# A spectral mixing layer with a gated feed-forward block: half spectrum as symmetric and antisymmetric channel parts, and three matmul passes per mirrored pair

## The chip, the cores and the metric

The kernel runs on one core of one Trainium2 chip. The metric is the device time of one execution in microseconds (us); the median of several executions is quoted. Most executions of one kernel here agree within 0.1%. Matmul inputs are bf16 (but for the folding of the weights in the change, which is fp32), sums are fp32, and the output is fp32.

Names of the engines in the profile: PE is the matmul engine, PEld its weight loads (they overlap with PE), DVE the vector engine, ACT the scalar engine, POOL the general engine that issues loads, SP the engine whose queue (SPq) issues stores.

## The reference

```python
# x: 8 x 3008 x 256
X = np.fft.fft(x, axis=1)            # over the 3008 positions
X = np.fft.fft(X, axis=2)            # over the 256 channels
y = X.real.reshape(24064, 256)
g = y @ w_gate                       # 256 -> 1536
gelu = 0.5 * g * (1 + erf(g / sqrt(2)))
out = (gelu * (y @ w_val)) @ w_out   # 1536 -> 256
```

Both kernels do the transform as matmuls: 3008 is factored as 47 x 64, and the channel transform is a product with a 256 x 256 table of cosines or sines. "Layer 1" below is the two products with w_gate and w_val, "layer 2" the product with w_out, "a feature block" 128 of the 1536 features (there are 12), and "the product" the elementwise gelu times value on DVE.

## The kernel before

For each batch it has five stages on PE: a 64-point transform over positions, 66 transposes on PE that turn the result, a 47-point transform, the channel transform (cosine part U and sine part V), and the feed-forward block. Because the input is real, only 33 of the 64 groups are computed; U + V gives one position and U - V the mirrored one. Both are written to SBUF, and the feed-forward block then treats all 3008 positions alike.

```python
# transposes, 8 per PSUM buffer: 94 elements of A with a step of K1H = 33
src = _sub(A, [[N2 * K1H, 2], [K1H, N2]], cc * AST + k1)
nc.tensor.transpose(pst[:, idx * 128 : idx * 128 + 128], src, ident)
...
# channel transform: direct and mirrored positions from U and V
nc.scalar.activation(vsb[:, :N], psV[:, :N], AF.Copy)
nc.vector.tensor_tensor(dstD, psU[:, :N], vsb[:, :N], op=ALU.add)
...
nc.vector.tensor_tensor(dstM, psU[:, off : off + Nm], vsb[:, off : off + Nm], op=ALU.subtract)
...
# layer 1, one feature block of a chunk of 512 positions: 2 + 2 matmuls
for t in range(NCH):
    nc.tensor.matmul(psg[:, :ntok], Wg_sb[:, t, fc*128:(fc+1)*128],
                     Yt[:, t, u0:u0+ntok], start=(t == 0), stop=(t == NCH - 1))
...                                    # the same into psv with Wv_sb
nc.scalar.activation(gl[:, :ntok], psg[:, :ntok], AF.Gelu)
nc.vector.tensor_tensor(h[:, fc, :ntok], gl[:, :ntok], psv[:, :ntok], op=ALU.mult)
...
# layer 2: 12 matmuls of 256 columns for 128 positions, then one store
# for each run of at most 47 positions
```

The order of the instructions on each engine is fixed when the kernel is built, but it is not exactly the order of the program: in the trace single layer-2 matmuls stand between those of layer 1, where the program has twelve in a row.

Of the kernel before, what the change touches and what calls it, by code (L numbers as in the profile page):

```python
# [27 lines left out]

@with_exitstack
def kernel(  # L30
# [12 lines left out]
    N1, N2 = 64, 47  # L43
    K1H = 33
    NCH = C // 128
    NFC = F // 128
    AST = 2 * N2 * K1H
    DIR = K1H * N2

    TOK = 512  # L50
    chunk_sizes = []
    t0 = 0
    while t0 < T:
        chunk_sizes.append(min(TOK, T - t0))
        t0 += TOK
    NCHUNKS = len(chunk_sizes)

    const_pool = ctx.enter_context(tc.tile_pool(name="const", bufs=1))
    psum_pool = ctx.enter_context(tc.tile_pool(name="psum", bufs=1, space=bass.MemoryType.PSUM))

    G2 = const_pool.tile([128, 24, 2 * 66], BF16)
    T_PQ = const_pool.tile([2 * N2, 2 * N2], BF16)
    C2_sb = const_pool.tile([128, NCH, C], BF16)
    S2_sb = const_pool.tile([128, NCH, C], BF16)
    ident = const_pool.tile([128, 128], BF16)
    Wg_sb = const_pool.tile([128, NCH, F], BF16)
    Wv_sb = const_pool.tile([128, NCH, F], BF16)
    Wo_sb = const_pool.tile([128, NFC, C], BF16)

    scr_a = const_pool.tile([128, 24, K1H], FP32)  # L70
    scr_b = const_pool.tile([128, 24, K1H], FP32)
    scr_c = const_pool.tile([128, 24, K1H], FP32)
    scr_d = const_pool.tile([128, 24, K1H], FP32)
    col_a = const_pool.tile([128, 1], FP32)
    col_b = const_pool.tile([128, 1], FP32)
    col_c = const_pool.tile([128, 1], FP32)
    row_j = const_pool.tile([128, 24], FP32)
    row_t = const_pool.tile([128, 24], FP32)
    row_k = const_pool.tile([128, K1H], FP32)

    work_pool = ctx.enter_context(tc.tile_pool(name="work", bufs=1))
# [3 lines left out]
    def x_tile():  # L85
        return work_pool.tile([128, 24, C], BF16, tag="x", bufs=2, name="x_sb")

    def load_x(b, groups=None):
        xt = x_tile()
        x_tiles.append(xt)  # L90
        if groups is None:
            groups = [(j0, 3) for j0 in range(0, 24, 3)]
        for (j0, gj) in groups:
            src = ap_replace(
                x,
                ap=[[N2 * C, N1], [C, gj], [1, C]],
                offset=x.offset + (b * T + j0) * C,
            )
            nc.gpsimd.dma_start(out=xt[0:N1, j0 : j0 + gj, :], in_=src)  # L99
            gj2 = min(gj, 23 - j0)  # L100
            if gj2 > 0:
                src = ap_replace(
                    x,
                    ap=[[N2 * C, N1], [C, gj2], [1, C]],
                    offset=x.offset + (b * T + 24 + j0) * C,
                )
                nc.gpsimd.dma_start(  # L107
                    out=_sub(xt, [[C, gj2], [1, C]], j0 * C, part_start=N1, part_num=N1),
                    in_=src,
                )  # L110

    def A_tile():
        return work_pool.tile([128, NCH, 2, N2, K1H], BF16, tag="A", bufs=1, name="A_sb")

    def Ap_tile():
        return work_pool.tile([2 * N2, K1H, C], BF16, tag="Ap", bufs=1, name="Ap_sb")

    def PQ_tile():
        return work_pool.tile([128, NCH, K1H, 2, N2], BF16, tag="PQ", bufs=1, name="PQ_sb")

    def Y_tile():
        return work_pool.tile([128, NCH, T], BF16, tag="Y", bufs=2, name="Y_sb")

    def h_tile():
        return work_pool.tile([128, NFC, TOK], BF16, tag="h", bufs=2, name="h_sb")

    def gelu_tile():
        return work_pool.tile([128, TOK], BF16, tag="gelu", bufs=3, name="gelu_sb")

    def osb_tile():  # L130
        return work_pool.tile([128, C], FP32, tag="osb", bufs=4, name="out_sb")

    def vsb_tile():
        return work_pool.tile([128, 10 * N2], BF16, tag="vsb", bufs=2, name="v_sb")

    def ps_l1():
        return psum_pool.tile([128, TOK], FP32, tag="l1", bufs=3, name="ps_l1")

    def ps_o():
        return psum_pool.tile([128, 2 * C], FP32, tag="o", bufs=1, name="ps_o")  # L140

    def ps_dft():
        return psum_pool.tile([128, 512], FP32, tag="dft", bufs=3, name="ps_dft")

    def ps_tr():
        return psum_pool.tile([2 * N2, 1024], BF16, tag="tr", bufs=1, name="ps_tr")

    nc.gpsimd.iota(col_a, pattern=[[0, 1]], base=0, channel_multiplier=1,
                   allow_small_or_imprecise_dtypes=True)
    nc.gpsimd.iota(row_j, pattern=[[1, 24]], base=0, channel_multiplier=0,  # L150
                   allow_small_or_imprecise_dtypes=True)
    nc.gpsimd.iota(row_k, pattern=[[1, K1H]], base=0, channel_multiplier=0,
                   allow_small_or_imprecise_dtypes=True)
    load_x(0, groups=[(0, 1), (1, 1), (2, 1)] + [(j0, 3) for j0 in range(3, 24, 3)])
    for w_hbm, w_sb in ((moe_w_gate, Wg_sb), (moe_w_val, Wv_sb)):
        for q in range(4):
            src = ap_replace(
                w_hbm,
                ap=[[F, 32], [128 * F, NCH], [1, F]],
                offset=w_hbm.offset + q * 32 * F,  # L160
            )
            nc.gpsimd.dma_start(
                out=_sub(w_sb, [[F, NCH], [1, F]], 0, part_start=q * 32, part_num=32),
                in_=src,
            )
    for q in range(4):
        src = ap_replace(
            moe_w_out,
            ap=[[C, 32], [128 * C, NFC], [1, C]],
            offset=moe_w_out.offset + q * 32 * C,  # L170
        )
        nc.gpsimd.dma_start(
            out=_sub(Wo_sb, [[C, NFC], [1, C]], 0, part_start=q * 32, part_num=32),
            in_=src,
        )
    make_identity(nc, ident)

    nc.vector.memset(_sub(G2, [[1, 3 * 132]], 0), 0.0)
    nc.vector.memset(_sub(G2, [[1, 21 * 132]], 3 * 132), 0.0)
    nc.vector.tensor_scalar(col_b, col_a, 64.0, -2984.0, op0=ALU.is_ge, op1=ALU.mult)  # L180
    nc.vector.scalar_tensor_tensor(col_c, col_a, 47.0, col_b, op0=ALU.mult, op1=ALU.add)
    nc.vector.tensor_scalar(row_t, row_j, col_c, 1.0 / T, op0=ALU.add, op1=ALU.mult)

    def g2_group(j0, nj):
        for j in range(j0, j0 + nj):
            nc.vector.tensor_scalar(scr_a[:, j, :], row_k, row_t[:, j : j + 1], None, op0=ALU.mult)
        pha = _sub(scr_a, [[K1H, nj], [1, K1H]], j0 * K1H)
        tmp = _sub(scr_b, [[K1H, nj], [1, K1H]], j0 * K1H)
        nc.vector.tensor_scalar(tmp, pha, MAGIC, None, op0=ALU.add)
        nc.vector.scalar_tensor_tensor(  # L190
            _sub(scr_c, [[K1H, nj], [1, K1H]], j0 * K1H), tmp, MAGIC, pha,
            op0=ALU.subtract, op1=ALU.subtract)
        for half in range(2):
            p0 = half * 64
            cb = half * 66
            nc.scalar.activation(
                _sub(G2, [[132, nj], [1, K1H]], j0 * 132 + cb + K1H, part_start=p0, part_num=64),
                _sub(scr_c, [[K1H, nj], [1, K1H]], j0 * K1H, part_start=p0, part_num=64),
                AF.Sin, scale=TWO_PI,
            )  # L200
        nc.vector.tensor_scalar(pha, pha, 0.25, None, op0=ALU.add)
        nc.vector.tensor_scalar(tmp, pha, MAGIC, None, op0=ALU.add)
        nc.vector.scalar_tensor_tensor(
            _sub(scr_d, [[K1H, nj], [1, K1H]], j0 * K1H), tmp, MAGIC, pha,
            op0=ALU.subtract, op1=ALU.subtract)
        for half in range(2):
            p0 = half * 64
            cb = half * 66
            nc.scalar.activation(  # L209
                _sub(G2, [[132, nj], [1, K1H]], j0 * 132 + cb, part_start=p0, part_num=64),  # L210
                _sub(scr_d, [[K1H, nj], [1, K1H]], j0 * K1H, part_start=p0, part_num=64),
                AF.Sin, scale=-TWO_PI,
            )

    g2_group(0, 3)
    g2_group(3, 9)
    g2_group(12, 12)

    def gen_tpq():
        pcol = col_a  # L220
        rifl = _sub(col_b, [[1, 1]], 0, part_num=2 * N2)
# [38 lines left out]

    rowk2_94 = const_pool.tile([2 * N2, 2, N2], FP32)
    qrow_94 = const_pool.tile([2 * N2, 2, N2], FP32)
    row256 = const_pool.tile([128, C], FP32)

    Y_bufs = [None] * B

# [317 lines left out]
```

## Time and profile before

Before: 1007.57 us, median of 4 runs (1007.52 to 1008.25).

The first two lines and the summary of the chain of waits on the page of the kernel before. The second line gives busy microseconds, share of the span and instruction count for each engine.

```profile
span 1006.3 us, 17363 instructions
...
PE 950.6 (94%) x6218; PEld 611.2 (61%) x6304; DVE 611.0 (61%) x1209; ACT 489.7 (49%) x941; POOL 76.7 (8%) x157
...
PE 86%; ACT 4%; DMA 4%; DVE 2%; issue 1%; SPq 1%; POOL 1%; ACTq 0%; POOLq 0%
```

PE is the limit: it is busy for 94% of the span, and 86% of the chain that ended last is PE.

Groups of instructions of the kernel before, by line. The columns are line, engine and operation, output and inputs with shapes, count, then busy us and mean ns of one, then idle time before them.

```profile
L479 PE MATMUL ps_o<-Wo_sb,h_sb 128*128 128x256 bf16 (+1 forms) x2304 | 296.2, 272 | 5.2 <-ACT out_sb L487 1.4
...
L329 PEld LDWEIGHTS <-A_sb 128*94 128x94 bf16 x528 | 94.3, 252 | 14.8 <-issue 9.4
L329 PE MATMUL ps_tr<-ident,A_sb 128*94 128x128 bf16 x528 | 90.9, 318 | 9.9 <-DVE Ap_sb L337 5.7 <-POOL ident masks.py:199 3.7
```

The mean time of one matmul includes its latency, since matmuls are pipelined; the time that matters is from one start to the next. The transposes stand out: their weight loads take 252 ns against about 100 for the others.

Long pieces of the chain of waits of the kernel before, in order of time: start, duration, what.

```profile
90.78 1.47 PE ps_o L479 x12
...
209.29 1.49 PE ps_o L479 x12
...
327.82 1.49 PE ps_o L479 x12
...
446.34 1.49 PE ps_o L479 x12
```

The same layer-2 group comes back every 118.5 us. That is the period of one batch, and the kernel's time is a start, eight batches and a tail.

Windows of the kernel before around its end: the stretch, its length, then busy time and count of each engine, clock, DMA share of 16 engines and GB/s. The clock is the share of full speed that PE was granted.

```profile
960.00:988.00 28.00, 26.24 (x168) 16.07 (x165) 12.27 (x20) 12.78 (x26) 0.00 (x0) 1.00 0.10 34
988.00:1006.00 18.00, 0.23 (x3) 0.00 (x0) 0.00 (x0) 0.38 (x1) 0.00 (x0) 0.60 0.08 26
```

The last 18 us are stores, at 26 GB/s; the last matmul ends at 988.2.

### The profile page before, as it was taken

To read this page: it belongs to the slowest core of one execution; us is meant where nothing else is said; L and a number is where in the kernel's file an instruction comes from. 1 tells how busy PE (TensorE), PEld (TensorE's weight loads), DVE (VectorE), ACT (ScalarE), POOL (GpSimd) and SP (SyncE) were. 2 spreads that over 40 slices of the span, in tenths; PEclk is the share of its full clock that TensorE was granted. 3 is DMA by queue.
4 is the path that set the end of the run, shared out by engine and by line. 5 is a ranking of instruction groups with operands and counts; after the bars stand their busy time and mean duration, and the time that the engine had idled before them with its cause. 6 is when DMAs were issued, how large, how long until landed. Compare 5 with 4: busy or idle time off the path is not lost.

```text
span 1006.3 us, 17363 instructions
## 1 busy us (share of the span) xinstructions
PE 950.6 (94%) x6218; PEld 611.2 (61%) x6304; DVE 611.0 (61%) x1209; ACT 489.7 (49%) x941; POOL 76.7 (8%) x157
## 2 busy tenths in 40 slices
PE   3699999999999999999999999999999999999992
PEld 2646666557655676566765577656765667555551
DVE  5566656675566647757575756667467564765550
ACT  4254544554455454545445554454445545455550
POOL 7600300003000020002100030000000000000000
PEclk9999999999999999999999999999999999999997
DMA  8901411015100151013210150101010110001110
GB/s 137 142 1 30 77 38 29 24 29 84 29 30 27 28 84 29 26 28 64 51 30 23 31 84 28 30 27 29 23 29 29 25 31 23 29 22 31 33 34 27
DMA packets 40190, 40.45 MB, mean 40 GB/s; under 512 B 5544, under 2 KB 39592, under 8 KB 40104
## 3 DMA queue, kind: packets, MB, share of 16 engines
q0 software_dynamic: 12800, 14.69, 9.9%
q1 hardware_dynamic: 27304, 24.65, 8.6%
q8 instruction: 49, 0.80, 0.3%
q14 instruction: 37, 0.30, 0.1%
HBM read 29.36 MB, written 24.64 MB: 54 GB/s over the span
## 4 chain that ended last, share of the span: by engine, by line
PE 86%; ACT 4%; DMA 4%; DVE 2%; issue 1%; SPq 1%; POOL 1%; ACTq 0%; POOLq 0%
PE ps_o L479 24%; PE ps_tr L329 8%; DMA out_dram<-out_sb 2%; PE ps_dft L389 2%; PE ps_dft L397 2%; ACT gelu_sb L463 2%; PE ps_dft L361 1%; ACT out_sb L487 1%; PE ps_dft L282 1%; SPq L508 1%; DMA Wg_sb<-in_moe_w_gate_dram 1%; DVE h_sb L464 1%; ACT Ap_sb L334 0%; DMA x_sb<-in_x_dram 0%; DVE PQ_sb L369 0%
## 5 line engine op out<-in xcount | busy, mean ns | idle before, releaser
L479 PE MATMUL ps_o<-Wo_sb,h_sb 128*128 128x256 bf16 (+1 forms) x2304 | 296.2, 272 | 5.2 <-ACT out_sb L487 1.4
L479 PEld LDWEIGHTS <-h_sb 128*128 128x128 bf16 (+1 forms) x2304 | 225.9, 99 | 72.1 <-issue 11.6
L455 PEld LDWEIGHTS <-Wv_sb 128*128 128x128 bf16 x1152 | 113.3, 99 | 113.7 <-issue 3.2
L487 ACT ACTIVATE out_sb<-ps_o 128x256 f32<-128x256 f32 x192 | 73.7, 384 | 204.1 <-PE ps_o L479 192.5
L446 PEld LDWEIGHTS <-Wg_sb 128*128 128x128 bf16 x1152 | 109.3, 98 | 99.1 <-issue 32.4
L329 PEld LDWEIGHTS <-A_sb 128*94 128x94 bf16 x528 | 94.3, 252 | 14.8 <-issue 9.4
L329 PE MATMUL ps_tr<-ident,A_sb 128*94 128x128 bf16 x528 | 90.9, 318 | 9.9 <-DVE Ap_sb L337 5.7
L303 DVE CAST A_sb<-ps_dft 128x198 bf16<-128x198 f32 (+2 forms) x254 | 75.2, 342 | 21.7 <-PE ps_dft L282 16.5
L99 POOL DMA_DIRECT2D x_sb<-in_x_dram x66 | 36.7, 556 | 514.6 <-PE ps_dft L290 386.4
L334 ACT ACTIVATE Ap_sb<-ps_tr 94x512 bf16<-94x512 bf16 (+1 forms) x72 | 40.1, 557 | 67.1 <-PE ps_tr L329 67.1
L337 DVE COPY Ap_sb<-ps_tr 94x512 bf16<-94x512 bf16 (+1 forms) x72 | 28.5, 396 | 66.7 <-ACT Ap_sb L334 66.7
L369 DVE CAST PQ_sb<-ps_dft 128x470 bf16<-128x470 f32 (+1 forms) x112 | 67.5, 612 | 1.8 <-PE ps_dft L361 1.8
L282 PE MATMUL ps_dft<-G_61,x_sb 128*128 128x132 bf16 x368 | 45.1, 231 | 12.5 <-ACT G_61 L209 10.1
L407 DVE TENSOR_TENSOR Y_sb<-ps_dft,v_sb 128x470 bf16<-128x470 f32 (+1 forms) x64 | 35.8, 560 | 29.5 <-ACT v_sb L405 29.5
L282 PEld LDWEIGHTS <-x_sb 128*128 128x128 bf16 x368 | 31.8, 102 | 32.0 <-DMA x_sb<-in_x_dram 8.1
L361 PEld LDWEIGHTS <-Ap_sb 94*128 94x128 bf16 x528 | 35.4, 103 | 20.5 <-issue 1.6
L361 PE MATMUL ps_dft<-T_PQ,Ap_sb 94*128 94x94 bf16 x528 | 41.5, 214 | 2.6 <-ACT T_PQ L241 1.0
L405 ACT ACTIVATE v_sb<-ps_dft 128x470 bf16<-128x470 f32 (+1 forms) x64 | 31.6, 494 | 22.4 <-PE ps_dft L397 15.7
L107 POOL DMA_DIRECT2D x_sb<-in_x_dram x66 | 36.9, 559 | 6.4 <-DMA x_sb<-in_x_dram 2.6
L389 PE MATMUL ps_dft<-PQ_sb,C_sb 128*128 128x470 bf16 (+1 forms) x128 | 35.0, 337 | 1.9 <-DVE Y_sb L418 0.7
L397 PE MATMUL ps_dft<-PQ_sb,S_sb 128*128 128x470 bf16 (+1 forms) x128 | 35.0, 336 | 0.0
L418 DVE TENSOR_TENSOR Y_sb<-ps_dft,v_sb 128x470 bf16<-128x470 f32 (+2 forms) x64 | 34.0, 531 | 0.0
(2358 smaller groups left out, 1460.2 us busy)
## 6 DMA issues: line engine op xcount, KB each, us to landing
out_dram<-out_sb SPq DMA_DIRECT2D x328, 47.0 KB
x_sb<-in_x_dram POOLq DMA_DIRECT2D x118, 96.0 KB, 5.4
Wg_sb<-in_moe_w_gate_dram POOLq DMA_DIRECT2D x4, 192.0 KB, 6.5
Wv_sb<-in_moe_w_val_dram POOLq DMA_DIRECT2D x4, 192.0 KB, 8.2
Wo_sb<-in_moe_w_out_dram POOLq DMA_DIRECT2D x4, 192.0 KB, 7.5
x_sb<-in_x_dram POOLq DMA_DIRECT2D x8, 64.0 KB, 5.3
out_dram<-out_sb SPq DMA_DIRECT2D x8, 46.0 KB
out_dram<-out_sb SPq DMA_DIRECT2D x8, 45.0 KB
```

Of the source, the lines that this page charges most:

```text
L282: nc.tensor.matmul(ps[:, jj * 132 : (jj + 1) * 132], xt[:, j, cc * 128 : (cc + 1) * 128], G2[:, j, :], start=True, stop=True,)
L303: nc.vector.tensor_copy(dst, src)
L329: nc.tensor.transpose(pst[:, idx * 128 : idx * 128 + 128], src, ident)
L334: nc.scalar.activation(dst, pst[:, :h1], AF.Copy)
L361: nc.tensor.matmul(ps[:, j * 94 : (j + 1) * 94], Ap[:, k1, cc * 128 : (cc + 1) * 128], T_PQ, start=True, stop=True,)
L369: nc.vector.tensor_copy(dst, ps[:, : g * 94])
L389: nc.tensor.matmul(psU[:, :N], C2_sb[:, t, cpj * 128 : (cpj + 1) * 128], _sub(PQ, [[2 * N2, g], [1, N2]], t * AST + a * 2 * N2), start=(t ...
L397: nc.tensor.matmul(psV[:, :N], S2_sb[:, t, cpj * 128 : (cpj + 1) * 128], _sub(PQ, [[2 * N2, g], [1, N2]], t * AST + a * 2 * N2 + N2), star ...
L446: nc.tensor.matmul(psg[:, :ntok], Wg_sb[:, t, fc * 128 : (fc + 1) * 128], Yt[:, t, u0 : u0 + ntok], start=(t == 0), stop=(t == NCH - 1),)
L455: nc.tensor.matmul(psv[:, :ntok], Wv_sb[:, t, fc * 128 : (fc + 1) * 128], Yt[:, t, u0 : u0 + ntok], start=(t == 0), stop=(t == NCH - 1),)
L479: nc.tensor.matmul(pso[:m, col0 : col0 + C], h[:, fc, sub * 128 : sub * 128 + m], Wo_sb[:, fc, :], start=(fc == 0), stop=(fc == NFC - 1),)
L487: nc.scalar.activation(osb[:m], pso[:m, col0 : col0 + C], AF.Copy)
```

## The change

The intent: the real part of the spectrum at a position and at its mirror are E + O and E - O, where E is symmetric in the channels and O antisymmetric. So 128 rows hold all of E and 128 rows all of O (row 0 of the O tile carries one extra symmetric channel). The weights are folded once, at the start, into W_E and W_O. Layer 1 of a position is then W_E E + W_O O. For its mirror one does not start afresh: a third matmul adds W_M O, with W_M = -2 W_O (and 0 in the row of the extra symmetric channel), onto the bank that already holds the first sum. That is three passes for two positions instead of four. The transform itself becomes 94-row stage-1 matmuls, the channel transform, and a 64-point stage whose outputs are E and O; its order makes the transposes unnecessary.

```diff
-                    src = _sub(A, [[N2 * K1H, 2], [K1H, N2]], cc * AST + k1)
-                    nc.tensor.transpose(pst[:, idx * 128 : idx * 128 + 128], src, ident)
 ...
+        for (nm, q) in folds:                       # 6 pieces, at the start
+            nc.tensor.matmul(ps, exch, w_hi[nm][:, fs], start=True, stop=True)      # fp32
+            nc.vector.scalar_tensor_tensor(W[nm,"E"][:, fs], ps, keep, lo, op0=ALU.mult, op1=ALU.add)
+            nc.vector.scalar_tensor_tensor(W[nm,"O"][:, fs], lo, keep, ps, op0=ALU.mult, op1=ALU.subtract)
+            nc.vector.tensor_scalar(W[nm,"M"][:, fs], W[nm,"O"][:, fs], keep2, None, op0=ALU.mult)
 ...
-                for t in range(NCH):
-                    nc.tensor.matmul(psg[:, :ntok], Wg_sb[...], Yt[...], ...)
+    # l1_first(ci, fc): chunk of 512 (or 481) positions of the half spectrum
+                for nm, ps in (("g", pg), ("v", pv)):
+                    nc.tensor.matmul(ps[:, :n], W[nm,"E"][:, fs], EO[:, 0, c0:c0+n], start=True, stop=False)
+                    nc.tensor.matmul(ps[:, :n], W[nm,"O"][:, fs], EO[:, 1, c0:c0+n], start=False, stop=True)
+                nc.scalar.activation(gl[:, :n], pg[:, :n], AF.Gelu)
+                nc.vector.tensor_tensor(h[:, fc, 0, :n], gl[:, :n], pv[:, :n], op=ALU.mult)
+    # l1_second(ci, fc): the mirrored positions, in the same two banks
+                for nm, ps in (("g", pg), ("v", pv)):
+                    nc.tensor.matmul(ps[:, :n], W[nm,"M"][:, fs], EO[:, 1, c0:c0+n], start=False, stop=True, ...)
+                nc.scalar.activation(gl[:, :n], pg[:, :n], AF.Gelu)
+                nc.vector.tensor_tensor(h[:, fc, 1, n-1::-1], gl[:, :n], pv[:, :n], op=ALU.mult)
 ...
+    # a feature block's slot: first[fc], transform of the next batch ("filler"),
+    # second[fc-1], layer 2 of the chunk before ("pend")
 ...
-                    ap=[[N1 * C, ln], [1, C]]                   # store: ln <= 47 positions
+                    ap=[[C, n2], [N2 * C, hi - lo], [1, C]]     # store: n2 = 2 times 64 positions
 ...
-                ap=[[N2 * C, N1], [C, gj], [1, C]]              # load of x: 64 partitions
+                ap=[[NJ * C, NP], [1, nj * C]]                  # load of x: NP = 94 partitions
```

(The code lines are shortened, and the rest of the new transform and of its tables is cut.) PSUM: two banks for gate, two for value, two for layer 2, two for the transform.

## The prediction

> **What bounds it now.** TensorE. The page gives PE busy 950.6 us of a span of 1006.3 (94%), DVE 61%, ACT 49%, and the chain of waits is 86% PE. Three parts: a start of 56 us before layer 1, eight batches, a store tail (last matmuls at 988, end at 1006). In the timeline the same layer-2 group returns every 118.6 us (90.8, 209.3, 327.8, 446.3): one batch.
>
> **Cost of one batch on PE.** Start-to-start times in the timeline: 512 columns 215 ns, 256 columns 109 ns, 132 columns 58 ns, transposes 162 ns. The first three agree with the Trainium skill ("TensorE: Matmul & The Clock Gate", Back-to-back issue gap: N/2.4 + 2.5 ns warm). Layer 1 (288 matmuls) 61 us, layer 2 (288) 31.4, transposes (66) 10.8, the rest of the transform about 11: 114 us. The other 4.5 us (4%) are stalls.
>
> **Removed, added, moved.** Layer 1 falls from 288 matmuls over 3008 columns to 216 over 1505 mirrored columns: 45.7 us by the same rule, saving 15. The transposes go (10.8 us). New transform: 64 matmuls of 96 columns, 48 of 256, 24 of 64 and 24 of 128: about 11 us, equal to the old one without transposes. Layer 2 stays at 31.4. Sum 88 us a batch, 26 less.
>
> Nothing moves off PE: gelu (597 ns for 512) and the product (687 ns) stay 72 of each. DVE per batch: 49 us of products plus about 15 of PSUM copies = 65; ACT: 43 of gelu plus about 15 = 58.
>
> New dependency: a gate/value bank pair is now held through matmul, gelu, product, correction matmul, gelu, product. By the durations about 2.7 us for the value bank; with two banks 1.35 us per feature block at best, against 2.45 us of PE work; but in program order the block's 1.8 us of DVE work lies in that loop (2.5 us with matmul latency). So I expect more stalls than now: 6-7%, 94 us per batch.
>
> **Ends.** Start: the transform of batch 0 needs all of x, and its load uses 94 partitions. The Trainium skill ("DMA: Bandwidth & Descriptors", Why a DMA increments its semaphore by 16) says a DMA uses the largest number of engines up to 16 that divides the outer dimensions, so 2 for 94; no run here shows it. The weights (fp32) load beside it, then are folded on DVE. I estimate first layer 1 at 50 us, and 5 us lost waiting for batch 1's x. Tail: 26 large stores a batch instead of 87 small ones; 6 us after the last matmul instead of 18.
>
> **Sum:** 50 + 5 + 7 x 94 + 81 (last batch, no transform beside it) + 6 = 800 us; 8 in 10 between 772 and 845. Faster by over 2%: 0.97, within 2%: 0.02, slower: 0.01.
>
> **What would show it.** Period of a layer-2 group 92-97 us; PE still above 90% busy in mid-span; layer-1 matmul count 1728; no transposes; DVE about 70% busy, ACT about 62%; SP queue issues about 208. If the bank loop binds, PE's waits will name DVE products and ACT gelu, and the period will be over 100.
>
> **What would make it wrong.** The bank loop binding (period 100-105, total 850 or more); x arriving late over few DMA engines (start 65 or later, stalls at each batch's first transform); strided PSUM reads or 4-byte writes in the stage-1 copy slower than 0.55 us; a better overlap than I assume (period 90, total 770).

## The result, and the profile after

After: 781.16 us, median of 4 runs (780.76 to 781.40), against 1007.57 before in the same session. The ratio is 0.7751 (95% interval 0.7740 to 0.7762). Ratios here are the mean time of one kernel's fast runs over that of the other's in the same rounds, so they are not quite the ratio of the medians quoted.

The same lines of the page of the kernel after:

```profile
span 779.6 us, 13835 instructions
...
PE 736.1 (94%) x5324; PEld 478.9 (61%) x5324; DVE 496.7 (64%) x872; ACT 437.8 (56%) x823; POOL 12.7 (2%) x29
...
PE 85%; DVE 5%; ACT 4%; issue 2%; DMA 1%; SPq 0%; ACTq 0%; POOL 0%; POOLq 0%; DVEq 0%
```

PE is the limit as before, with the same busy share. Groups of the kernel after, by line:

```profile
L461 PE MATMUL ps_o<-Wo_sb,h_sb 128*128 128x256 bf16 (+1 forms) x2304 | 298.4, 273 | 0.0
...
L425 PE MATMUL ps_g<-EO_sb,WgE 128*128 128x512 bf16 (+1 forms) x288 | 107.8, 374 | 2.9 <-ACT gelu_sb L445 0.4
...
L441 PE MATMUL ps_g<-EO_sb,WgM 128*128 128x512 bf16 (+1 forms) x288 | 108.3, 376 | 0.8 <-ACT gelu_sb L428 0.7
```

Layer 2 is what it was. Layer 1 has six such groups of 288 (E, O and M, for gate and value): 1728 matmuls instead of 2304. The transposes are gone. The chain of waits in order of time:

```profile
89.58 1.31 PE ps_o L461 x12
...
179.81 1.31 PE ps_o L461 x12
...
270.03 1.31 PE ps_o L461 x12
```

The period is 90.2 us. Windows of the kernel after, for one load of x in mid-span, and around the end (columns as above):

```profile
168.60:180.30 11.70, 11.67 (x83) 7.90 (x81) 7.80 (x13) 6.14 (x11) 0.00 (x0) 1.00 0.73 141
756.00:765.00 9.00, 7.00 (x65) 6.32 (x62) 0.00 (x0) 1.19 (x2) 0.00 (x0) 1.00 0.14 48
765.00:774.00 9.00, 0.00 (x0) 0.00 (x0) 0.00 (x0) 0.60 (x1) 0.00 (x0) 0.57 0.20 64
774.00:780.00 6.00, 0.00 (x0) 0.00 (x0) 0.00 (x0) 0.00 (x0) 0.00 (x0) 0.50 0.08 28
```

While x is loaded, 0.73 of 16 engines are busy, that is 11.7 (the few stores of this stretch are counted too). Near the end, from 756 to 765, 0.14 of 16, that is 2.2, move 48 GB/s; PE works until 763.0 and then has nothing left to do, while 0.20 and then 0.08 of 16 engines (3.2 and 1.3) finish the stores. The end of the chain of waits of the kernel after shows the same:

```profile
755.18 0.61 ACT out_sb L470
...
755.80 0.51 SPq L407
...
756.36 9.48 DMA out_dram<-out_sb
...
765.95 0.60 ACT out_sb L470
```

The last copy of layer 2 on ACT needs a buffer that a store gives free; this store takes 9.5 us, and the copy starts at 765.95, 2.9 us after the last matmul.

The terms of the predicted sum beside the trace (first layer-1 matmul, end of the last matmul, end of the span):

| part | predicted, us | trace of after, us |
|---|---|---|
| start, to the first layer-1 matmul | 50 | 45.1 |
| from there to the end of the last matmul | 744 (5 + 7 x 94 + 81) | 717.9 |
| tail, to the end of the span | 6 | 16.6 |
| sum | 800 | 779.6 |

The period of the middle batches, taken from the first product of one batch to that of the next (the mean of six), is 90.33 us after and 118.57 before. If one adds N/2.4 + 2.5 ns for each matmul of a batch of the kernel after, the sum is 87.1 us; the start-to-start times of the trace, which has every matmul in this run, exceed that by 3.2 us a batch. This excess is what is left to stalls.

### The profile page after: what moved, and what is told of

Read it like the earlier page. It is cut to its first block, busy times and chain, and to the rows that moved or that the text cites. A ratio compares the mean times of both kernels' runs of the same rounds, so it can differ in the third digit from the quotient of the medians.

```text
span 779.6 us, 13835 instructions
## 1 busy us (share of the span) xinstructions
PE 736.1 (94%) x5324; PEld 478.9 (61%) x5324; DVE 496.7 (64%) x872; ACT 437.8 (56%) x823; POOL 12.7 (2%) x29
## 4 chain that ended last, share of the span: by engine, by line
PE 85%; DVE 5%; ACT 4%; issue 2%; DMA 1%; SPq 0%; ACTq 0%; POOL 0%; POOLq 0%; DVEq 0%
PE ps_o L461 30%; PE ps_g L425 9%; PE ps_v L425 8%; PE ps_v L426 8%; PE ps_g L426 7%; PE ps_v L441 7%; PE ps_g L441 7%; PE ps_dft L314 6%; PE ps_dft L285 3%; ACT gelu_sb L445 2%; DMA out_dram<-out_sb 1%; DVE h_sb L447 1%; PE ps_dft L356 1%; DVE h_sb L429 1%; ACT out_sb L470 1%
## 5 line engine op out<-in xcount | busy, mean ns | idle before, releaser
L429 DVE TENSOR_TENSOR h_sb<-gelu_sb,ps_v 128x512 bf16<-128x512 bf16 (+1 forms) x288 | 195.0, 677 | 204.2 <-ACT gelu_sb L428 132.4
L428 ACT ACTIVATE gelu_sb<-ps_g 128x512 bf16<-128x512 f32 (+1 forms) x288 | 169.7, 589 | 163.8 <-PE ps_g L426 163.4
L447 DVE TENSOR_TENSOR h_sb<-gelu_sb,ps_v 128x512 bf16<-128x512 bf16 (+1 forms) x288 | 193.1, 671 | 42.0 <-ACT gelu_sb L445 40.2
L445 ACT ACTIVATE gelu_sb<-ps_g 128x512 bf16<-128x512 f32 (+1 forms) x288 | 169.1, 587 | 41.7 <-PE ps_g L441 40.9
L425 PE MATMUL ps_g<-EO_sb,WgE 128*128 128x512 bf16 (+1 forms) x288 | 107.8, 374 | 2.9 <-ACT gelu_sb L445 0.4
L425 PE MATMUL ps_v<-EO_sb,WvE 128*128 128x512 bf16 (+1 forms) x288 | 107.8, 374 | 1.3 <-DVE h_sb L447 0.6
L441 PE MATMUL ps_g<-EO_sb,WgM 128*128 128x512 bf16 (+1 forms) x288 | 108.3, 376 | 0.8 <-ACT gelu_sb L428 0.7
L441 PE MATMUL ps_v<-EO_sb,WvM 128*128 128x512 bf16 (+1 forms) x288 | 108.0, 375 | 0.6
L426 PE MATMUL ps_v<-EO_sb,WvO 128*128 128x512 bf16 (+1 forms) x288 | 108.1, 375 | 0.0
L426 PE MATMUL ps_g<-EO_sb,WgO 128*128 128x512 bf16 (+1 forms) x288 | 108.0, 375 | 0.0
L470 ACT ACTIVATE out_sb<-ps_o 128x512 f32<-128x512 f32 x96 | 57.3, 597 | 82.2 <-PE ps_o L461 75.3
L285 PE MATMUL ps_dft<-G,x_sb 94*128 94x96 bf16 x512 | 46.2, 212 | 19.9 <-ACT G L183 10.8
L314 PE MATMUL ps_dft<-CS,A_sb 128*128 128x256 bf16 x384 | 60.7, 280 | 0.9 <-DVE Z_sb L324 0.6
## 6 DMA issues: line engine op xcount, KB each, us to landing
x_sb<-in_x_dram POOLq DMA_DIRECT2D x14, 752.0 KB, 11.8
```

The source lines that it names most:

```text
L285: nc.tensor.matmul(ps[:, jj * 96 : (jj + 1) * 96], xt[:, j0 + jj, cc * 128 : (cc + 1) * 128], G[:, j0 + jj, :], start=True, stop=True,)
L314: nc.tensor.matmul(ps[:, d * C : (d + 1) * C], A[:, cc, k2 + d, :], CS[:, cc, :], start=(cc == 0), stop=(cc == 1),)
L425: nc.tensor.matmul(ps[:, :n], W[nm, "E"][:, fs], EO[:, 0, c0 : c0 + n], start=True, stop=False)
L426: nc.tensor.matmul(ps[:, :n], W[nm, "O"][:, fs], EO[:, 1, c0 : c0 + n], start=False, stop=True)
L428: nc.scalar.activation(gl[:, :n], pg[:, :n], AF.Gelu)
L429: nc.vector.tensor_tensor(st["h"][:, fc, 0, :n], gl[:, :n], pv[:, :n], op=ALU.mult)
```

## The experiments

Periods below are means over the same six batches. The runs of one group were made on one chip; before took 1007.66, 1007.67 and 1007.74 us there, so times can be set beside each other across groups within a few tenths.

### 1. Four passes again: how much the third pass saves

```diff
-   nc.vector.tensor_scalar(keep2, keep, -2.0, None, op0=ALU.mult)
+   nc.vector.tensor_scalar(keep2, keep, -2.0, 1.0, op0=ALU.mult, op1=ALU.add)   # W_M = -W_O
 ...
-   nc.tensor.matmul(ps[:, :n], W[nm,"M"][:, fs], EO[:, 1, c0:c0+n], start=False, stop=True, ...)
+   nc.tensor.matmul(ps[:, :n], W[nm,"E"][:, fs], EO[:, 0, c0:c0+n], start=True, stop=False)
+   nc.tensor.matmul(ps[:, :n], W[nm,"M"][:, fs], EO[:, 1, c0:c0+n], start=False, stop=True)
```

> Undoes the three-pass part alone: the second product of a mirrored pair starts afresh with E and minus O (4 matmuls per pair and weight instead of 3); the new transform, the banks and the elementwise work stay. Theory A (TensorE columns set the period): 72 more matmuls of about 211 ns a batch, period 90.2 + 15.2 = 105.4 us, time 781 + 122 = 903 us (895-910). Rival B (the period is set by the two-bank loop through gelu and product, PE has slack in it): the period grows by less than half of that, time under 845.

Measured: 890.64 us, correct, ratio to before 0.8837; period 104.41. So the gain of 226 us splits into 117 for all else that changed, that is the new transform, its schedule, its start and its stores (1007.7 to 890.6), and 109.5 for the third pass (890.6 to 781.2). The period grew by 14.1 us and not by the 15.2 of the added matmuls, because the excess fell from 3.2 to 2.1 us: with more PE work per block, PE waits less for the banks. PE's columns set the period, as theory A says, but the third pass gave back 1.1 us a batch in new waits, and the time falls short of theory A's lower limit of 895 by 4 us.

### 2. Half of what the transposes cost was the way they read

```diff
 # in the kernel before; wrong result on purpose
-   src = _sub(A, [[N2 * K1H, 2], [K1H, N2]], cc * AST + k1)
+   src = _sub(A, [[1, 2 * N2]], cc * AST + k1 * 2 * N2)
```

> Wrong result on purpose: in the kernel before, each transpose reads 94 consecutive elements of A instead of 94 with a step of 33 (66 bytes); count, shapes and all else stay. It asks what made the removed transposes 162 ns apart (their weight loads 252 ns, against 100 for the others). Theory A (the strided weight read): loads fall to about 100 ns, pitch to 60-100, 66 x 60-100 ns = 4-7 us a batch, time 955-975. Rival B (a transpose of 94 columns is that slow in itself): load and pitch within 10%, time 1003-1010.

Measured: 967.59 us (ratio 0.9602; the result is wrong, as intended), period 113.18 instead of 118.57. The groups of this run, to be set beside those of the kernel before (252 and 318 ns):

```profile
L329 PE MATMUL ps_tr<-ident,A_sb 128*94 128x128 bf16 x528 | 44.5, 229 | 9.0 <-DVE Ap_sb L337 5.9 <-POOL ident masks.py:199 2.7
L329 PEld LDWEIGHTS <-A_sb 128*94 128x94 bf16 x528 | 41.6, 131 | 19.4 <-issue 10.5
```

From start to start the transposes take 56 ns instead of 162 (medians). So 5.4 us a batch of what the change removes is the price of reading with a step of 66 bytes, not of transposing. The Trainium skill ("SBUF — State Buffer", the note on cachelines in the section on the DMA port swizzle) says that SBUF has lines of 16 bytes and that each access to a new line costs extra; that fits this run. The kernel before could have had a third of the transform's gain (40 of 117 us, if such a layout of A can be written, which was not tried).

### 3. The tail: stores over two DMA engines

```diff
-   n2 = 2 if i + 1 < len(segs) and segs[i + 1][0] == k2 + 1 else 1
+   n2 = 1
```

> One change to the kernel after: each store covers one row segment (64 tokens) instead of two neighbouring ones (2 x 64), so its outer dimension is 64 and not 2. Theory A (each store is carried by two DMA engines because its outer dimension is 2; the trace of after shows 2.2 engines busy and 48 GB/s while the last 1 MB drains, from 756 to 778 us): the drain is spread over up to 16 engines, the tail from the last layer-2 matmul (755) to the end (779.6) shrinks from 24 us to 6-9, time 764-768 us. Rival B (the tail is the completion latency of stores and their issue, about 0.5 us each, now twice as many): no gain, 778-785 us. The period of a batch stays 90.2 us in both.

Measured: 771.21 us, correct, ratio 0.7654. Windows of this run around its end:

```profile
755.00:765.00 10.00, 8.09 (x75) 7.30 (x72) 0.00 (x0) 2.39 (x4) 0.00 (x0) 1.00 0.39 94
765.00:770.00 5.00, 0.00 (x0) 0.00 (x0) 0.00 (x0) 0.00 (x0) 0.00 (x0) 0.52 0.14 37
```

The share of 0.39 is 6.2 engines, and they move 94 GB/s instead of 48. A store of 64 KB lands 2.1 us after its issue here (median, DMA view), where the store of 128 KB at the end of the chain above took 9.5. The time from the end of the last matmul to the end of the span falls from 16.6 to 6.5 us. Theory A holds, rival B falls; the period (90.36) did not move. The gain is 10 us and not the expected 13 to 17, because I had read the last matmul at 755 us; it ends at 763 in both kernels.

### 4. How long a bank is held

```diff
-   tag="g", bufs=2 ... tag="v", bufs=2
+   tag="g", bufs=1 ... tag="v", bufs=1
 ...  # in the slot of block fc
    first[fc]()
    (filler)
-   if fc > 0: second[fc - 1]()
    (pend)
+   second[fc]()
```

(A first form, with one bank but the old order of the slot, asks for a block's banks before the block before it has had its correction, and so can't run.)

> One bank for gate and one for value instead of two each, and the correction matmuls of a block in the block's own slot: the period then measures how long the value bank is held per feature block. Theory A (my prediction's estimate, 2.7 us held plus the start of the next block's matmuls): period 36 x 2.7 to 36 x 3.1 = 97-112 us, time 835-950. Rival B (the hold is much shorter, and that is why the loop did not bind): period under 94 us, time under 810. Rival C (much longer, over 3.3 us, and only the reordering of blocks hides it): time over 990.

Measured: 848.21 us, correct; period 96.89, or 2.69 us for each of the 36 blocks. One value bank in the timeline of this run (start, duration, engine and line, operation):

```profile
301.30 0.38 PE L425 MATMUL ps_v<-EO_sb,WvE 128*128 128x512 bf16 x1
301.51 0.38 PE L426 MATMUL ps_v<-EO_sb,WvO 128*128 128x512 bf16 x1
302.00 0.69 DVE L429 TENSOR_TENSOR h_sb<-gelu_sb,ps_v 128x512 bf16<-128x512 bf16 x1 [0.16 <-PE ps_dft L314]
302.74 0.38 PE L441 MATMUL ps_v<-EO_sb,WvM 128*128 128x512 bf16 x1
303.23 0.69 DVE L447 TENSOR_TENSOR h_sb<-gelu_sb,ps_v 128x512 bf16<-128x512 bf16 x1
304.08 0.38 PE L425 MATMUL ps_v<-EO_sb,WvE 128*128 128x512 bf16 x1
```

The bank is taken at 301.30 and given free at 303.92: 2.62 us, which is also the mean of the six middle batches; the prediction had 2.7. So that estimate was right for a correction that follows at once, as in this run. In the kernel after the program puts the correction into the next block's slot, and there the same reading of the trace gives 4.8 us from the start of a block's value E matmul to the end of its second product (mean of 216 blocks; the shortest is 3.3). What was too high is the stalls put down: two banks each make the excess 3.2 us a batch, not 6.

### 5. Is the rest of the excess a wait for banks?

```diff
-   tag="g", bufs=2 ... tag="v", bufs=2 ... tag="o", bufs=2 ... tag="dft", bufs=2
+   tag="g", bufs=3 ... tag="v", bufs=3 ... tag="o", bufs=1 ... tag="dft", bufs=1
```

> Three banks each for gate and value instead of two, paid for with one bank each for layer 2 and for the transform (two before). Theory A (what is left of PE's excess, 3.2 us a batch, is mostly the wait for a bank pair): the gaps behind the correction matmuls (1.2 us a batch behind the gate one) and behind the gate O matmuls (0.6) fall under 0.3 each; whether the time falls depends on what the single layer-2 and transform banks cost, so 775-790 us in all. Rival B (not bank waits): these two gaps stay above 0.8 us together.

Measured: 790.66 us, correct. The period fell to 89.10, so 1.2 us less; the excess behind the gate correction fell from 1.23 to 0.18 us a batch and that behind the gate O matmul from 0.64 to 0.02, as theory A expects. (This trace lacks 61 matmul records, so its other excesses are not read.) It is slower in all because the start grew: the first product of batch 0 comes at 72.0 us instead of 48.6, which fits the single transform bank, since batch 0's transform has nothing beside it to hide its copies; but the granted clock was also 0.50 from 26.6 to 60 us in this run (in the kernel after it was 1.00 again from 40 us on), and the two were not separated. The bank waits are real, but another split of the eight banks is not the cure.

### 6. More even filling alone: a miss

```diff
-   l2s = [l2_unit(ci, s, g) for s in range(nsub) for g in range(2)]          # 12 matmuls each
+   l2s = [l2_unit(ci, s, g, p) for s in range(nsub) for g in range(2) for p in range(3)]   # 4 each
```

> Emits layer 2 in pieces of 4 matmuls, so that each feature block gets 8 layer-2 matmuls as filling, instead of 12 in two blocks of three and none in the third. In the trace of after the excess of PE's start-to-start times over the bare streaming time is 3.3 us a batch, and half of it stands behind the correction matmuls of blocks without a layer-2 unit. Theory A (those blocks wait for the bank pair): excess falls to 1-1.5 us, period 88-88.7 us, time 764-770. Rival B (the excess is switching between weights and is not a bank wait): period 90 and time 779-783.

Measured: 787.62 us, correct, 6 us slower than the kernel after; period 91.73. Both expectations were wrong. The excess behind the correction matmuls vanished (gate 1.23 to 0.07, value 0.28 to 0.02 us a batch), but a new one came before the value matmuls of the next block. One block in the timeline of this run:

```profile
301.02 0.37 PE L441 MATMUL ps_g<-EO_sb,WgM 128*128 128x481 bf16 x1
...
301.23 0.60 ACT L346 ACTIVATE EO_sb<-ps_dft 128x512 bf16<-128x512 f32 x1
301.23 0.37 PE L441 MATMUL ps_v<-EO_sb,WvM 128*128 128x481 bf16 x1
...
301.43 1.04 PE L461 MATMUL ps_o<-Wo_sb,h_sb 128*128 128x256 bf16 x8
301.72 0.57 ACT L445 ACTIVATE gelu_sb<-ps_g 128x481 bf16<-128x481 f32 x1
302.32 0.66 DVE L447 TENSOR_TENSOR h_sb<-gelu_sb,ps_v 128x481 bf16<-128x481 bf16 x1 [0.55 <-ACT gelu_sb L445]
302.34 0.36 PE L425 MATMUL ps_g<-EO_sb,WgE 128*128 128x481 bf16 x1
...
302.54 0.36 PE L426 MATMUL ps_g<-EO_sb,WgO 128*128 128x481 bf16 x1
...
302.74 0.22 PE L356 MATMUL ps_dft<-TPI,Z_sb 128*128 128x128 bf16 x1
...
303.03 0.36 PE L425 MATMUL ps_v<-EO_sb,WvE 128*128 128x481 bf16 x1
```

The correction of a block starts at 301.02. Its gelu stands behind a transform copy on ACT and starts only at 301.72, the product ends at 302.98, and the next block's value matmul, which needs that bank, starts at 303.03. The PE work from the start of that correction is, by start-to-start times, two corrections (0.41), 8 layer-2 matmuls (0.87), two gate matmuls (0.41) and one of the transform (0.06): 1.7 us, where correction, gelu and product take 1.96. The shortest such stretch in this run is 1.67 us, so by this count the work would have been enough in this block without the copy in front of the gelu. Over all 216 blocks of the six middle batches correction, gelu and product take 1.89 us and the PE work before the next use of the value bank is 1.90, both means; in 81% of the blocks the next value matmul starts within 0.11 us of the product's end. Four more layer-2 matmuls would add 0.44 us. In the kernel after, the order on PE mostly shows two blocks of three with 12 layer-2 matmuls behind the correction and the third with none; that this is better in sum than even pieces is what the times show, why it is was argued and not tested.

### 7. The transform work behind the correction

```diff
    first[fc]()
-   (filler)
    if fc > 0: second[fc - 1]()
+   (filler)
    (pend)
```

> In each block the transform work is put behind the correction matmuls instead of before them: it then lies between a block's correction and the next matmuls into the same banks. Theory (a correction needs about 1.7 us of other PE work before the next value matmuls: 0.4 matmul, 0.6 gelu, 0.65 product; blocks without a layer-2 unit lack it): excess 3.2 falls to about 1.5-2 us a batch, period 88.5-89.3, time 767-775. Rival (the order in the program hardly matters, since the order on PE is rearranged when the kernel is built): 779-783.

> The even layer-2 pieces of e3 and the late transform work of e6 together. e3 was slower (787.6) because 8 layer-2 matmuls are 0.87 us, with the matmuls around them 1.5 us, less than the 1.7 us that a bank pair needs in every block. With the transform work there too it is about 1.8 us in every block: excess under 1.5 us a batch, period 88-88.5, time 764-770. Rival (e3 was slower for another reason, such as copies on ACT ahead of gelu): 782-790.

Measured: alone (e6) 776.79 us with a period of 89.72, which is 4.4 us better but short of the expected 767 to 775; together with the even pieces (e7) 762.91 us, ratio 0.7571, with a period of 87.99, inside what was expected. Both are correct. The pieces that made things worse alone (+6.5 us) make them better by 13.9 us when the transform work follows the correction. In e7 the period is 0.9 us above the sum of the bare matmul times, so the bank loop hardly binds any more. The move does two things at once: it adds PE work where the bank needs time, and it takes transform copies from in front of the gelu and product of the correction. No run separates them, but the traces of e3 and e7 show both. The PE work between a correction and the next use of its value bank rises from 1.90 to 2.11 us or more (mean; 61 matmul records are missing in e7). Correction, gelu and product take 1.89 us before and 1.90 after in the mean, while the median falls from 1.91 to 1.74. A next value matmul that starts within 0.11 us of the product's end is found in 81% of the blocks of e3 and in 23% of those of e7. By the means, then, the added PE work is the part that is seen; the rival of e7, copies in front of the gelu, is not excluded as a part of it.

### 8. The start

```diff
 # stage-1 copies, and likewise the copies of the channel transform
-   if (j0 // 4 + cc) % 4 == 3:                                    # to ACT, else DVE
+   if (j0 // 4 + cc) % (2 if b == 0 else 4) == (1 if b == 0 else 3):
```

> Only for batch 0, every second PSUM copy of the transform goes to ACT (one in four before). In the start PE waits 7.5 us (19 to 26.6 us) for a stage-1 copy that stands behind the weight folding on DVE, while ACT is idle. Theory A: the first layer-1 matmul moves from 45 us to 38-41, time 775-778. Rival B (the start is bound by the x load or by DVE's folding in any case): under 1.5 us gained.

Measured: 778.99 us, correct, 2.2 us better than after: between the two expectations. The first layer-1 matmul comes at 44.1 us instead of 45.1, where 38 to 41 had been expected; among runs with the same start (after, e1, e2, e3, e6, e7) it varies from 44.4 to 45.3. The reason is in the windows of the kernel after for its start:

```profile
0.00:19.00 19.00, 8.18 (x24) 3.81 (x25) 16.54 (x56) 10.11 (x12) 6.58 (x17) 1.00 0.96 259
19.00:26.60 7.60, 0.06 (x2) 0.00 (x0) 7.60 (x19) 0.62 (x2) 0.00 (x0) 0.70 1.20 212
26.60:45.00 18.40, 15.53 (x114) 10.51 (x114) 11.71 (x21) 4.33 (x8) 1.02 (x2) 0.66 0.57 111
```

From 19.0 to 26.6 us DVE is busy throughout with table and folding work, ACT has next to none, and PE waits: one of the two transform banks needs a DVE copy. As long as every second copy is a DVE copy, PE still waits for the first of them, as the timeline of e8 shows (6.42 us idle, ended by a DVE copy; it was 7.54 in the kernel after):

```profile
26.67 0.48 PE L285 MATMUL ps_dft<-G,x_sb 94*128 94x96 bf16 x4 [6.42 <-DVE A_sb L298]
```

The windows above also show, in the third column from the end, that the granted clock of PE (as a share of its full speed) was 0.66 from 26.6 to 45 us.

### 9. All that helped, together

```diff
 # e7 and n2 = 1, and for batch 0:
+   if b == 0 or (j0 // 4 + cc) % 4 == 3:        # all stage-1 copies of batch 0 on ACT
 # e11 in addition
-   nc.vector.tensor_scalar(W[nm, "M"] ...)
+   nc.gpsimd.tensor_scalar(W[nm, "M"] ...)
```

> The parts that helped, together: even layer-2 pieces, transform work behind the corrections (e7, 762.9), stores of one row segment (e1, 10 us off the tail), and for batch 0 all stage-1 copies on ACT and every second channel copy (e8 gained 2 us with half of the stage-1 copies). If the parts add, 762.9 - 10 - 2 to 5 = 748-751 us: period 88.0, first product at 44-47 us, tail from last matmul to end under 8 us. If the tail or the start share their gain with the reordering, 752-760.

> e9 with the third folding step of the weights (the correction weights, 6 operations of 0.35 us on DVE) on GpSimd. Theory (the start is bound by DVE: 26 of its first 27 us are busy): first product 1-2 us earlier than in e9, time 1-2 us less. Rival (GpSimd is slower on them and the first layer-1 matmuls wait for it, or DVE no longer binds): same as e9 or up to 4 us more.

Measured: e9 745.01 us (744.91 to 745.28), correct, ratio to before 0.7394; by the medians 36 us or 4.6% under the kernel after. It does better than expected: the first product of batch 0 comes at 40.6 us, 7.7 earlier than in e7 (48.3) where 2 to 5 had been expected, the period is 87.97, and 6.4 us pass from the end of the last matmul (736.8) to the end of the span (743.2). That the gain of the start came only when all stage-1 copies left DVE bears out the reading of experiment 8. How much of the 7.7 us is the wait itself is open: a window of e9 shows that PE also had a higher clock in the second part of the start, 0.86 from 26 to 45 us, where the kernel after had 0.66 from 26.6 to 45.

```profile
26.00:45.00 19.00, 15.88 (x128) 10.34 (x129) 10.20 (x21) 10.90 (x22) 0.53 (x2) 0.86 0.54 112
```

e11 took 744.75 us: 0.3 less, within the spread of the runs, so the third folding step on DVE was not what held the start any more. (In e9 DVE is busy for 23.5 of the first 27 us, not for the 26 that the expectation of e11 names.) e9 is the version to keep.

## Why the prediction was right

The prediction was 800 us (772 to 845), the time 781.2. Point by point:

- **PE is the limit, and the change takes 26 us of PE work out of each batch: right.** The period fell by 28.2 us (118.57 to 90.33). The parts: the third pass was put at 15 us and measured 14.1 in the period; the transform, put at 10.8 (the transposes), measured 14.2 (118.57 to 104.41), and experiment 2 shows that 5.4 of these are the strided weight reads. The start-to-start times behind the sum hold: 109 ns for 256 columns, 56 for 128, 42 for 96. By them the new transform sums to 10.0 us and not to about 11, and that is why the sum is 87.1 and not 88.
- **The bank loop: the mechanism right, its size wrong.** "So I expect more stalls than now: 6-7%, 94 us per batch." The hold of a value bank was estimated at 2.7 us and measured 2.62 where the correction follows at once (experiment 4); in the kernel after itself it is 4.8, which the estimate did not foresee. Banks do cause waits (experiments 5 to 7). But the term was mis-sized: 3.2 us a batch instead of 6, so the period was 90.3, under the predicted 92 to 97. I had taken the order of the program for the order on the engines. The build had rearranged it: in the trace the layer-2 matmuls and the corrections of two blocks stand together where the bank is not free yet. That this order is why the stalls were fewer is not shown; no run has two banks and the order of the program. Over seven periods this term is worth 26 us, more than the whole difference of 19.
- **"so 2 for 94": wrong.** In the Trainium skill ("DMA: Bandwidth & Descriptors", Why a DMA increments its semaphore by 16 and not by 1) the rule has an exception that I read over: loads whose descriptors are made in software by POOL may use all 16 engines, with some partitions on each. The trace shows 11.7 engines busy and 11.8 us from issue to landing for 752 KB. Hence also no wait for batch 1's x, the 5 us. That the start itself came near the 50 put down, at 45, is luck: batch 0's x had all landed by 18.8 us, and what held PE was DVE (experiment 8), which the prediction named as a part of the start but not as its limit.
- **The tail of 6 us: wrong by 10.6.** Here the same rule did apply and I had not applied it: most stores, issued by SP, have an outer dimension of 2, and 2.2 engines were busy from 756 to 765 us (2 by the rule; 3.2 in the next 9 us, when the last stores, of one row each, are among them). Fewer and larger stores were counted as a gain; they were one in issues (208 instead of 696), and the end of the kernel before shows still less, 26 GB/s, but it was not the gain put down. Experiment 3 shows it with one changed number.
- **The last batch of 81 us: too low.** It took 90.3 from its first product to the end of the last matmul. Layer 2 runs one chunk behind, so batch 0's period is short (82.0 us) and the last batch carries the rest; with the 3.5 us from the first layer-1 matmul to the first product, this is 4.5 us more than was put down.
- **Errors cancelled, and that was luck.** The two that made the prediction too high (stalls 26 us, start 10) outweighed the two that made it too low (tail 10.6, first and last batch 4.5). The range held, but the central value was right to 2.4% with four mis-sized terms.
- **What was to show it:** 1728 layer-1 matmuls, no transposes, PE above 90% and 208 stores came as said. DVE at 64% and ACT at 56% are somewhat under the 70% and 62% put down.

## What to carry to other kernels

When a change makes an accumulator live through two rounds of "matmul, activation, product", estimate how long the bank is held and how much other PE work the program has between the release that is needed and the matmul that needs it; then place that work there on purpose, because even layer-2 pieces made this kernel 6 us slower with the transform work before the correction, and 18 us faster with it behind. Look at the outermost dimension of each store's access pattern and not only at its size: two rows of 64 went out on two DMA engines, one row of 64 on more, and in the tail that was 10 us. And cost each instruction by start-to-start times in the trace with its own access pattern: more than a third of what the new transform saves per batch (5.4 of 14.2 us) was the stride of a read.

## What the Trainium skill lacked or had wrong

- "TensorE: Matmul & The Clock Gate", Back-to-back issue gap: the rule N/2.4 + 2.5 ns agrees with the streams of bf16 weight load and matmul pairs here (215 ns at 512 columns, 109 at 256, 56 at 128, 42 at 96, medians), except for the transposes of the kernel before with their strided weights. The sustained figures that the same section gives for such streams in a real kernel, about 131 ns at 512 and 81 at 128, do not: here it is never under 215 for 512, and 55 for 128.
- The same page, Part 4 on transposes: it gives some 275 ns for a transpose in a kernel and names the access latency. The runs show 318 ns for one and 162 from start to start with a source step of 66 bytes, 229 and 56 with a contiguous source; the section does not mention this difference.
- "DMA: Bandwidth & Descriptors", Why a DMA increments its semaphore by 16 and not by 1: the exception for software-made descriptors is given for "some direct copies" without saying which. Here a casting load of 94 partitions, 752 KB, had 11.7 of 16 engines busy (with the few stores beside it).
- "Trainium Kernel Development and Optimization", Performance Expectations, at Reading a trace: beside MFU it calls the busy share of weight loads a good measure of the distance to the limit. Here it was 61% before, 61% after and 64% in e9, whose period is within 1% of the sum of its matmul times; it did not tell these kernels apart.
